# Taking the first queries of a second batch ahead, and a rebuilt opening, in a fused attention and SwiGLU kernel

## The chip, the cores and the metric

The kernel runs on one core of one Trainium2 chip. The metric is the device time of one execution in microseconds (us). In the views PE is TensorE (PEld its weight loads), DVE VectorE, ACT ScalarE, POOL GpSimd and SP SyncE; FFN stands for the SwiGLU block. The kernel before takes 454.88 us (median of 4 runs, 454.54 to 455.0).

## The reference, cut to what matters

Eight batches of eight heads of causal attention with a decay, 576 tokens each, head size 64, feed a SwiGLU block over all 4,608 tokens (model width 512, inner width 1,536).

```python
scores = scale * np.matmul(q, k.transpose(0, 1, 3, 2))
cum = np.cumsum(np.log(np.clip(f, 0.0001, 1.0)), axis=-1)
scores = np.where(causal, -1e9, scores + cum[:, :, :, None] - cum[:, :, None, :])
attn = softmax(scores)                    # rows divided by their sums
x = (attn @ v) as [4608, 512]
out = (silu(x @ w_gate) * (x @ w_val)) @ w_out
```

A token's FFN needs all eight heads of its batch. So the first FFN matmul can only come when the first 256 queries of all eight heads of batch 0 are done. Until then TensorE has only attention, and attention needs the other engines as much as TensorE.

## The kernel before

The program is a list of **slots**, one per step of a head (four per head, 256 in all, then a tail). `at(slot, fn, ...)` puts a piece of work into a slot, every engine executes its own part in program order, and FFN matmuls are mixed in by a ration per slot. Heads go in pairs; `QK[p]` holds the transposed q and k of a pair, with four more rows for the decay, so that the score matmul adds the decay itself. Batch 0 is split: the first 256 queries of its eight heads come first (slots 0 to 7), the rest after.

```python
def rows(p):                                   # decay rows of a later pair, by way of DRAM
    nc.sync.dma_start(out=QK[p % NBUF][D:KR, :, :S],
                      in_=dec_dram[2 * p : 2 * p + 2].rearrange("j w r s -> r (j w) s"))
...
def turn(h, half):                             # batch 0: sums to columns on TensorE, reciprocal,
    ...                                        # and turn_back(): columns to rows, both fp32
def collect(g): ...                            # later batches: sums -> DMA -> reciprocal -> DMA -> broadcast
...
TILES = [(0, QSPLIT), (QSPLIT, MT - QSPLIT)] + [(t0, MT) for t0 in range(MT, N_TOK, MT)]   # 256, 256, 512, ...
...
# opening: the decay is computed for all 64 heads on VectorE, then
for r in range(4):                             # four copies, all batch 0 at once, after the last row is done
    nc.sync.dma_start(out=QKA[D + r : D + r + 1, :, :, :S]..., in_=dec[:H, :, r])
...
def slot(h, i):
    if h >= H:
        return NSLOT * h + i
    return h if i == 0 else H + (NSLOT - 1) * h + i - 1
...
for c in range(4):                             # weights in quarters, from GpSimd
    at(1 + 3 * c, weights, wg, w_gate, lo, hi, True)
    at(2 + 3 * c, weights, wv, w_val, lo, hi, True)
for c in range(4):
    at(15 + 3 * c, weights, wo, w_out, 3 * c, 3 * c + 3, False)
```

The softmax here doesn't subtract the row's maximum and nothing guards it: scores larger than these inputs give would overflow.

## Time and profile before

| what | value |
|---|---|
| time, median | 454.88 us |
| span of the profiled run | 454.3 us |
| TensorE busy | 418.7 us, 92% |
| first score matmul | 19.04 us |
| first FFN (gate) matmul | 37.36 us |
| steady part (slot 192 to 224, one batch) | 45.6 us |

The page of the kernel before, cut to TensorE, its granted clock and the DMA. A row of digits is the span in 40 slices of 11.4 us; a digit is a share in tenths.

```profile
span 454.3 us, 7863 instructions
...
PE 418.7 (92%) x2752; PEld 239.9 (53%) x2752; DVE 290.9 (64%) x504; ACT 264.4 (58%) x537; POOL 185.0 (41%) x418
...
PE   2399999878799999999999999999999999999996
...
PEclk9999999998899999999999999999999999999999
DMA  9799935482746275628462746274614023101002
```

TensorE is full except in the first two slices and around slices 8 to 11. Everything after is saturated, so whatever is to be gained lies before about 125 us.

The windows view of the kernel before, in stretches of 5 us: window, its length, then busy us and instruction count of TensorE, its weight loads, VectorE, ScalarE and GpSimd, then granted clock, DMA share and GB/s.

```profile
15.00:20.00 5.00, 0.96 (x8) 0.87 (x9) 1.62 (x4) 0.45 (x2) 0.00 (x0) 1.00 0.57 139
20.00:25.00 5.00, 4.43 (x33) 3.37 (x30) 3.15 (x6) 3.70 (x9) 4.75 (x11) 1.00 0.66 178
25.00:30.00 5.00, 4.57 (x28) 2.95 (x28) 3.98 (x12) 2.17 (x5) 4.87 (x14) 1.00 1.07 142
35.00:40.00 5.00, 5.00 (x29) 3.50 (x28) 2.13 (x6) 2.22 (x6) 2.51 (x6) 1.00 1.31 202
50.00:55.00 5.00, 5.00 (x47) 3.92 (x47) 4.00 (x11) 2.61 (x7) 3.18 (x7) 1.00 1.07 230
```

GpSimd is full from 20 to 30, and the DMA engines are full from 25 to 55 (a share over 1 means that packets overlap).

The timeline of TensorE in the kernel before: start, duration, line, operation, tiles, and in brackets the idle time before it and what ended it.

```profile
19.04 0.80 PE L157 MATMUL s<-QK 68*128 68x256 bf16 x4 [4.58 <-DMA QK<-dec]
...
37.36 1.04 PE L287 MATMUL gp<-xT,wg 128*128 128x256 bf16 x4
38.19 0.64 PE L296 MATMUL vp<-xT,wv 128*128 128x256 bf16 x2
...
39.09 0.38 PE L296 MATMUL vp<-xT,wv 128*128 128x256 bf16 x2
39.31 0.60 PE L287 MATMUL gp<-xT,wg 128*128 128x256 bf16 x4
```

The first score matmul waits 4.58 us for the decay rows. Two 256-wide matmuls take 0.64 us at 38.19 and 0.38 us at 39.09: TensorE ran at half rate until 39.0. The Trainium skill, "TensorE: Matmul & The Clock Gate", section "Seeing it yourself" in Part 1, warns not to trust the clock records fully; here the durations decide.

### The profile page before, as it was taken

How to read it: one execution, taken by the hardware profiler on the slowest of the kernel's cores; microseconds unless marked ns; L12 is line 12 of the kernel's file. 1: busy time of each engine (PE TensorE's matmuls, PEld its weight loads, DVE VectorE, ACT ScalarE, POOL GpSimd, SP SyncE). 2: the span in 40 equal slices, each digit the busy share in tenths (PEclk: the TensorE clock that was granted, in tenths of full speed). 3: DMA queues.
4: the chain of work that ended last, by engine and by line, in shares of the span. 5: the costliest groups of instructions: out<-in, count | busy, mean ns of one | idle time of the engine just before them, and what ended most of it. 6: DMA issues, size and time to landing. Idle time of an engine off the chain costs nothing.

```text
span 454.3 us, 7863 instructions
## 1 busy us (share of the span) xinstructions
PE 418.7 (92%) x2752; PEld 239.9 (53%) x2752; DVE 290.9 (64%) x504; ACT 264.4 (58%) x537; POOL 185.0 (41%) x418
## 2 busy tenths in 40 slices
PE   2399999878799999999999999999999999999996
PEld 1266756655455555555555555555555544444442
DVE  7575655764569656965696469646964783771770
ACT  5344657786577667666766676667666631332322
POOL 6493535665535354545454545454545200000000
PEclk9999999998899999999999999999999999999999
DMA  9799935482746275628462746274614023101002
GB/s 205 188 173 216 198 76 166 107 183 62 184 105 132 56 202 132 134 54 203 130 135 56 202 131 133 56 203 130 134 28 123 26 55 98 48 0 70 24 0 95
DMA packets 68728, 52.83 MB, mean 116 GB/s; under 512 B 44624, under 2 KB 63056, under 8 KB 67728
## 3 DMA queue, kind: packets, MB, share of 16 engines
q1 hardware_dynamic: 57552, 38.35, 33.5%
q10 hardware_dynamic: 5312, 9.26, 9.4%
q0 software_dynamic: 5824, 4.72, 7.0%
q8 instruction: 22, 0.36, 0.3%
q14 instruction: 18, 0.15, 0.1%
HBM read 46.67 MB, written 10.16 MB: 125 GB/s over the span
## 4 chain that ended last, share of the span: by engine, by line
PE 68%; DVE 15%; DMA 6%; issue 4%; ACT 4%; POOL 2%; POOLq 0%; DVEq 0%; ACTq 0%
PE fo L305 18%; PE gp L287 16%; PE vp L296 15%; PE s L157 7%; DMA rb<-rc_d 4%; DVE hh L298 3%; DVE QK L141 3%; DVE xT L269 3%; DVE th L290 3%; PE tp L134 3%; ACT th L289 1%; PE rs L239 1%; ACT QK L139 1%; ACT pt L163 1%; DMA lf<-in_f_dram 1%
## 5 line engine op out<-in xcount | busy, mean ns | idle before, releaser
L163 ACT ACTIVATE pt<-s 128x384 bf16<-128x384 f32 (+2 forms) x248 | 124.0, 503 | 70.4 <-PE s L157 66.1
L175 POOL TENSOR_SCALAR_AFFINE_SELECT pt<-pt 128x256 bf16<-128x256 bf16 (+2 forms) x248 | 86.3, 350 | 171.3 <-ACT pt L163 169.5
L296 PE MATMUL vp<-xT,wv 128*128 128x512 bf16 (+1 forms) x480 | 124.2, 358 | 0.9 <-DVE th L290 0.5
L287 PE MATMUL gp<-xT,wg 128*128 128x512 bf16 (+1 forms) x480 | 124.3, 360 | 0.5 <-DVE xT L269 0.5
L290 DVE SCALAR_TENSOR_TENSOR th<-th,gp 128x512 f32<-128x512 f32 (+1 forms) x120 | 75.8, 631 | 63.6 <-ACT th L289 62.8
L305 PE MATMUL fo<-wo,hh 128*128 128x512 bf16 x432 | 107.7, 382 | 0.0
L289 ACT ACTIVATE th<-gp 128x512 f32<-128x512 f32 (+1 forms) x120 | 66.4, 554 | 56.3 <-PE gp L287 49.5
L157 PE MATMUL s<-QK 68*128 68x320 bf16 (+4 forms) x448 | 89.4, 271 | 4.6 <-DMA QK<-dec 4.6
L298 DVE TENSOR_TENSOR hh<-th,vp 128x512 bf16<-128x512 f32 (+1 forms) x120 | 75.5, 629 | 6.2 <-PE vp L296 0.9
L157 PEld LDWEIGHTS <-QK 68*128 68x128 bf16 x448 | 44.9, 101 | 46.5 <-issue 5.9
L141 DVE COPY QK<-tp 64x576 bf16<-64x576 bf16 x64 | 48.2, 753 | 29.9 <-PE tp L134 29.3
L296 PEld LDWEIGHTS <-wv 128*128 128x128 bf16 x480 | 45.3, 98 | 36.6 <-issue 2.5
L269 DVE TENSOR_TENSOR xT<-ev,rb 64x576 bf16<-64x576 f32 x56 | 45.1, 805 | 30.4 <-DMA rb<-rc_d 29.8
L287 PEld LDWEIGHTS <-wg 128*128 128x128 bf16 x480 | 44.9, 98 | 33.9 <-issue 0.7
L305 PEld LDWEIGHTS <-hh 128*128 128x128 bf16 x432 | 40.4, 98 | 35.8
L139 ACT ACTIVATE QK<-tp 64x576 bf16<-64x576 bf16 x64 | 41.2, 644 | 2.4 <-PE tp L134 1.9
L308 ACT ACTIVATE ot<-fo 128x512 f32<-128x512 f32 x36 | 21.5, 596 | 36.0 <-PE fo L305 29.7
L193 PEld LDWEIGHTS <-VB_101 128*128 128x128 bf16 x112 | 9.6, 101 | 12.8 <-PE s L157 5.7
L122 POOL CAST b_k_100<-nat_k 96x768 bf16<-96x768 f32 x16 | 16.2, 1012 | 0.0
L134 PE MATMUL tp<-ident,b_q_97 128*128 128x128 bf16 x96 | 9.0, 236 | 5.4 <-POOL b_q_97 L122 5.4
L193 PEld LDWEIGHTS <-VB_103 128*128 128x128 bf16 x112 | 9.6, 98 | 8.1 <-issue 2.4
L122 POOL CAST b_k_99<-nat_k 96x768 bf16<-96x768 f32 x16 | 13.4, 837 | 1.1 <-DMA nat_k<-in_k_dram 1.1
(344 smaller groups left out, 349.6 us busy)
## 6 DMA issues: line engine op xcount, KB each, us to landing
nat_q<-in_q_dram SPq DMA_DIRECT2D x32, 288.0 KB
nat_k<-in_k_dram SPq DMA_DIRECT2D x32, 288.0 KB
out_dram<-ot SPq DMA_DIRECT2D x36, 256.0 KB
nat_v<-in_v_dram SPq DMA_DIRECT2D x64, 128.0 KB
rb<-rc_d ACTq DMA_DIRECT2D x14, 576.0 KB
wg<-in_moe_w_gate_dram POOLq DMA_DIRECT2D x4, 384.0 KB, 7.9
wv<-in_moe_w_val_dram POOLq DMA_DIRECT2D x4, 384.0 KB, 8.6
wo<-in_moe_w_out_dram POOLq DMA_DIRECT2D x4, 384.0 KB, 6.2
```

The source lines that it names most:

```text
L139: nc.scalar.activation(dst, sr, AF.Copy)
L141: nc.vector.tensor_copy(dst, sr)
L157: nc.tensor.matmul(s[:, c : c + w], QK[b][:, 2 * j + 1, kt * P : (kt + 1) * P], QK[b][:, 2 * j, q0 : q0 + w], start=True, stop=True,)
L163: nc.scalar.activation(pt[:, off : off + c], s[:, :c], AF.Exp, scale=0.125)
L175: nc.gpsimd.affine_select(out=diag, in_=diag, pattern=[[1, m]] if m else [[0, 2], [1, P]], compare_op=ALU.is_ge, fill=0.0, base=0, channel ...
L269: nc.vector.tensor_mul(xT[a * D : (a + 1) * D, (h % H) // 2, b0 : b0 + S], E[g][:D, j], RB[g][:, j])
L287: nc.tensor.matmul(g_[:, :n], wg[:, ko, fs], xT[:, ko, ts], start=(ko == 0), stop=(ko == KD - 1))
L289: nc.scalar.activation(th[:, :n], g_[:, :n], AF.Tanh, scale=0.5)
L290: nc.vector.scalar_tensor_tensor(out=th[:, :n], in0=th[:, :n], scalar=1.0, in1=g_[:, :n], op0=ALU.add, op1=ALU.mult)
L296: nc.tensor.matmul(v_[:, :n], wv[:, ko, fs], xT[:, ko, ts], start=(ko == 0), stop=(ko == KD - 1))
L298: nc.vector.tensor_mul(h_[:, :n], th[:, :n], v_[:, :n])
L305: nc.tensor.matmul(o[:m], hh[fc][:, m0 : m0 + m], wo[:, fc, :], start=(fc == 0), stop=(fc == KF - 1))
```

## The change

Its intent: start attention sooner, keep TensorE warm with dummy matmuls, take work from GpSimd in the first heads, and split batch 1 as batch 0 is split, so that FFN tiles of 256 tokens are ready early and fill the stretch in which attention alone cannot fill TensorE. The core of the diff (helper bookkeeping cut, and with it a changed order of the casts, transposes and normalisations of the later batches):

```diff
+AHEAD = 2
...
+    def idle(n):                       # dummy matmuls of 512 columns into a spare PSUM tile
+        for _ in range(n):
+            z = ps_ffn.tile([P, MT], F32, name="z", tag="f")
+            nc.tensor.matmul(z, ident, ident.unsqueeze(1).to_broadcast([P, MT // P, P]), start=True, stop=True)
...
-    def turn(h, half):                 # fp32 transposes for both parts of batch 0
+    def turn(h):                       # for its first part alone; the second goes through the DMA chain
...
-    TILES = [(0, QSPLIT), (QSPLIT, MT - QSPLIT)] + [(t0, MT) for t0 in range(MT, N_TOK, MT)]
+    TILES = [(0, QSPLIT), (QSPLIT, QSPLIT), (2 * QSPLIT, QSPLIT), (3 * QSPLIT, AHEAD * S - 3 * QSPLIT)]
+    TILES += [(t0, min(MT, N_TOK - t0)) for t0 in range(AHEAD * S, N_TOK, MT)]
...
+        def row(r):                    # pair 0 alone, each row when it is computed
+            nc.sync.dma_start(out=QK[0][D + r : D + r + 1, :, :S], in_=dec[0:2, :, r])
...
+        row(3)
+        nc.sync.dma_start(out=dec_dram[:H], in_=dec[:H])
...
+        load(3, "q")
+        load(3, "k")
+        for part in range(3):
+            load(2, "v", part)
+        rows(1)                        # pairs 1 to 3 by way of DRAM
+        rows(2)
+        rows(3)
...
-        for r in range(4):
-            nc.sync.dma_start(out=QKA[D + r : D + r + 1, ...], in_=dec[:H, :, r])
...
+        nc.sync.dma_start(out=dec_dram[H:], in_=dec[H:])
...
     def slot(h, i):
-        if h >= H:
+        if h >= AHEAD * H:
             return NSLOT * h + i
-        return h if i == 0 else H + (NSLOT - 1) * h + i - 1
+        b, j = h // H, h % H
+        return NSLOT * H * b + (j if i == 0 else H + (NSLOT - 1) * j + i - 1)
...
+    for part in range(3):
+        at(0, load, 3, "v", part)
+    for n in range(first):
+        at(n, idle, 1)
...
-        at(1 + 3 * c, weights, wg, w_gate, lo, hi, True)
-        at(2 + 3 * c, weights, wv, w_val, lo, hi, True)
+        at(-1 + 3 * c, weights, wg, w_gate, lo, hi, True)
+        at(0 + 3 * c if c else -1, weights, wv, w_val, lo, hi, True)
```

## The prediction

> **What bounds it now.** The page gives TensorE 418.7 busy of 454.3 us (92%), so the time is TensorE's work plus the stretches where it waits or runs slow. Windows and timeline show four stages.
> 1. 0 to 19.0 us: no real matmul. The first score matmul waits for four copies of decay rows into QK, which start only after the VectorE chain ends at 12.1 us and take from 11.6 to 17.2 to issue.
> 2. 19.0 to 37.4: first queries of batch 0, up to the first gate matmul. GpSimd is saturated (9.6 of 10 us from 20 to 30), and TensorE is cold: four 256-wide gate matmuls take 1.04 us at 37.4, 0.60 soon after. The Trainium skill, "TensorE: Matmul & The Clock Gate", Part 1, says that the array runs at half rate until about 3.4 us of sustained work; these durations agree, although the granted-clock column says 1.0.
> 3. 37.4 to 123.9 (first 512-wide FFN tile): FFN work is rationed, 256 tokens over 48 program slots. Attention alone sets 0.92 us per slot (7.35 us per two heads). From 60 to 125 TensorE idles about 10.5 us, and the granted clock falls to 0.73 (105 to 110) and 0.66 (120 to 125), about 3 us more. VectorE waits for the broadcast reciprocals (1.4 and 4.0 us) begin the worst gaps.
> 4. From 123.9: regular, 45.56 us per batch (1.42 per slot), TensorE 98.8% busy. The change leaves this rate alone.
>
> **What the change does.**
> - Pair 0's rows go out singly, for two heads, as each is computed: first score matmul at about 15 instead of 19 (-4).
> - GpSimd loses, in the first heads, one of two masks per head, two blankings and two casts; 40 dummy matmuls (8.5 us if warm) keep TensorE warm. First gate matmul at about 29.5, some 14.5 us of first heads instead of 18.4 (-4).
> - Batch 0's second parts use the DMA chain instead of fp32 transposes on TensorE. Timeline starts give 0.25 + 0.49 us per head: -6.
> - Batch 1's first 256 queries go ahead; the first tiles are 256, 256, 256, 384. Counted in the built instruction streams, FFN work per slot becomes 0.38 us (slots 12-52), 0.96 (52-84), 0.60 (84-122), then 0.96 as before. Only the first stays under the 0.92 us attention limit. Estimate from 0.92 and 1.42: slot 52 near 68, 84 near 114, 122 near 155, where before it was at 176 (123.9 + 37 x 1.42), with 3 us more FFN done. Idle and throttle of stage 3 shrink by about 8 us.
> - FFN columns stay equal (276.5 us at full rate); 256-wide matmuls start every 0.11 us, so small tiles cost TensorE nothing.
>
> **Sum.** -4 -4 -6 -8 and -2 for cold FFN matmuls: -24. All of it is on the critical path, as TensorE is saturated afterwards. Predicted 430.5 us, 8 in 10 between 421 and 441. Faster by over 2%: 0.94; within: 0.05; slower: 0.01.
>
> **What would show it.** First score matmul 14 to 16 us; first gate matmul 28 to 31; 256-wide gate groups of four at about 0.6 from the start; TensorE idle between 40 and 130 under 6 us; clock 1.0 throughout; steady period still 45.5 us; tail after the last matmul still 3.6 us.
>
> **What would make it wrong.** Weights and batch 1's loads share the DMA with the new sum chains at 40 to 60 us, where DMA is already full (share over 1 from 25 to 55): the in-order VectorE would wait for reciprocals and stop everything, and the clock could drop. Pair 1's rows go through DRAM and may be late (1 to 3 us). If slots 12-52 run at 1.1 us, 7 us are lost.

## More of the kernel before

The DMA issues of the weights in the kernel before: count, KB of one, and median us from issue to landing.

```profile
wg<-in_moe_w_gate_dram POOLq DMA_DIRECT2D x4, 384.0 KB, 7.9
wv<-in_moe_w_val_dram POOLq DMA_DIRECT2D x4, 384.0 KB, 8.6
wo<-in_moe_w_out_dram POOLq DMA_DIRECT2D x4, 384.0 KB, 6.2
```

## The result, and the profile after

The changed kernel takes 452.43 us (median; 451.59, 452.25 and 452.6 in its fast runs). The ratio to the kernel before is 0.9941, with a 95% interval of 0.9922 to 0.9961: the same within 2%. It is 22 us above the prediction and 11 us above its upper end. Every ratio here is the mean time of one kernel's fast runs over that of the kernel before in the same rounds, so it is not quite the ratio of the medians that are quoted beside it.

One of the changed kernel's runs, the profiled one, took 723.46 us at a granted clock of 0.559. It was in the slow state, it is not explained, and no comparison below uses it; all 72 runs of the experiments were fast. The profile after is that of a second, fast profiled execution of the unedited changed kernel (the run `e1_again`, span 450.9 us).

The page of the changed kernel, the same rows:

```profile
span 450.9 us, 8053 instructions
...
PE 416.5 (92%) x2803; PEld 247.2 (55%) x2840; DVE 290.0 (64%) x523; ACT 267.5 (59%) x551; POOL 174.3 (39%) x409
...
PE   7399387899899899999999999999999999999996
...
PEclk9879889999999999999999999999999999999999
DMA  9899961670818554943584359435922222100201
```

The holes of slices 8 to 11 are smaller, but there are two new ones: a 3 in the second slice and a 3 in the fifth. The clock row dips beside both.

The windows of the changed kernel, the same columns:

```profile
15.00:20.00 5.00, 0.23 (x2) 0.00 (x0) 0.45 (x1) 0.73 (x2) 4.71 (x12) 0.85 1.03 254
20.00:25.00 5.00, 4.60 (x28) 3.18 (x28) 2.10 (x4) 2.74 (x6) 4.45 (x8) 0.50 0.85 117
25.00:30.00 5.00, 5.00 (x32) 3.32 (x31) 3.79 (x10) 2.54 (x6) 1.84 (x4) 0.63 1.25 214
...
50.00:55.00 5.00, 0.00 (x0) 0.00 (x0) 0.00 (x0) 0.36 (x1) 0.86 (x2) 0.76 1.15 225
```

TensorE does nothing from 15 to 20 and again from 50 to 55, with the DMA full both times; from 20 to 28.7 it runs at half rate. GpSimd is relieved only from 25 on (1.84 instead of 4.87 us).

The timeline of TensorE in the changed kernel at the lines that answer to those of before:

```profile
13.95 0.34 PE L166 MATMUL s<-QK 68*128 68x256 bf16 x2 [1.66 <-DMA QK<-dec]
...
20.40 0.48 PE L166 MATMUL s<-QK 68*128 68x256 bf16 x2 [5.17 <-DMA QK<-dec_d]
...
36.59 0.60 PE L293 MATMUL gp<-xT,wg 128*128 128x256 bf16 x4
...
55.34 0.80 PE L135 MATMUL tp<-ident,b_k 128*128 128x128 bf16 x6 [6.03 <-ACT QK L142]
```

The first pair starts 5 us sooner, at 13.95. The second pair then waits 5.17 us for its own decay rows, which come through DRAM (`dec_d`), and starts at 20.40, where it was before. The first gate matmul comes at 36.59 instead of 37.36.

The other new hole ends at 55.34. ScalarE, which TensorE waited for, in the timeline:

```profile
54.06 0.53 ACTq L250 DMA_DIRECT2D sc<-ev  x1
54.64 0.65 ACT L142 ACTIVATE QK<-tp 64x576 bf16<-64x576 bf16 x1 [5.63 <-DMA nat_q<-in_q_dram]
```

And GpSimd, in the timeline:

```profile
54.14 0.82 POOL L122 CAST b_q<-nat_q 96x768 bf16<-96x768 f32 x1 [4.92 <-DMA nat_q<-in_q_dram]
```

And the chain of waits over that stretch (start, us, what):

```profile
41.58 12.41 DMA nat_q<-in_q_dram
...
54.06 0.53 ACTq L250
...
54.64 0.66 ACT QK L142
...
55.34 0.80 PE tp L135 x6
```

All three name one transfer: the q of a pair of batch 1, issued at 41.58, took 12.41 us to land; the median of such loads over the run is 3.9 us. GpSimd needs it for its next cast. ScalarE does not need its data at all there: it stands at the issue of a DMA of its own (`sc<-ev`), because the semaphore that this issue takes in the built program is one that the earlier load still holds. The trace shows it: the load of 41.58 and the issue at 54.06 carry the same semaphore, and ScalarE waits for it just before the issue. ScalarE works in order, so its copy of a TensorE result (to `QK`) behind that issue waits, and TensorE behind the copy.

The DMA issues of the weights in the changed kernel:

```profile
wg<-in_moe_w_gate_dram POOLq DMA_DIRECT2D x4, 384.0 KB, 11.6
wv<-in_moe_w_val_dram POOLq DMA_DIRECT2D x4, 384.0 KB, 13.6
wo<-in_moe_w_out_dram POOLq DMA_DIRECT2D x4, 384.0 KB, 9.4
```

Each weight quarter takes 3 to 5 us longer than before. Batch 1's loads are not the main reason: in e9, an experiment told below in which batch 1 is not ahead, the quarters take nearly as long. No run isolates what the reason is.

```profile
wg<-in_moe_w_gate_dram POOLq DMA_DIRECT2D x4, 384.0 KB, 10.8
wv<-in_moe_w_val_dram POOLq DMA_DIRECT2D x4, 384.0 KB, 12.2
wo<-in_moe_w_out_dram POOLq DMA_DIRECT2D x4, 384.0 KB, 9.8
```

### Where each kernel stands at the same program slot

The start of a slot is read from the trace as the first weight load of its score matmuls, counted in program order. FFN work done is the count of FFN columns issued by then, at 2,400 columns per us; the trace agrees to about 1% (six 512-wide matmuls take 1.46 us and one 0.38 us, so five more take 0.216 us each, 2,370 per us). The last three columns are experiments told below. Every column is one profiled execution, and the four runs of one version differ by 1 to 4.4 us in whole time, so a difference of a few tenths of a us between columns says nothing.

| at slot | before | changed | predicted | batch 1 not ahead (e9) | mended (e17) | mended, batch 1 not ahead (e18) |
|---|---|---|---|---|---|---|
| 0, us | 19.0 | 14.0 | 15 | 13.8 | 13.3 | 14.0 |
| 12, us | 36.5 | 36.0 | 29.5 | 36.7 | 32.3 | 33.0 |
| 52, us | 85.5 | 85.3 | 68 | 79.7 | 78.9 | 74.1 |
| 84, us | 118.7 | 135.0 | 114 | 115.5 | 128.6 | 109.3 |
| 122, us | 176.0 | 178.5 | 155 | 167.8 | 172.1 | 161.4 |
| 255, us | 364.4 | 365.0 | | 353.8 | 357.8 | 347.1 |
| FFN done by slot 52, us | 20.2 | 15.4 | | 15.4 | 15.4 | 15.4 |
| FFN done by slot 84, us | 30.5 | 46.1 | | 32.6 | 46.1 | 32.6 |
| FFN done by slot 122, us | 66.3 | 69.1 | | 66.6 | 69.1 | 66.6 |
| whole time, us | 454.88 | 452.43 | 430.5 | 447.97 | 446.28 | 440.35 |

(The prediction's 29.5 is for the first gate matmul, which is at slot 12 to within 1 us.) The changed kernel reaches slot 122 2.5 us later than the kernel before, with 2.8 us more FFN work behind it. Up to there the whole change is worth nothing. The little it gains comes afterwards: slots 122 to 255 take 186.4 us instead of 188.4.

### The profile page after: what moved, and what is told of

Its sections match the earlier page's. It is cut to its first block, busy times and chain, and to the rows that moved or that the text cites. A ratio compares the mean times of both kernels' runs of the same rounds, so it can differ in the third digit from the quotient of the medians.

```text
span 721.7 us, 8090 instructions
## 1 busy us (share of the span) xinstructions
PE 711.6 (99%) x2840; PEld 341.5 (47%) x2840; DVE 300.0 (42%) x523; ACT 276.5 (38%) x551; POOL 170.1 (24%) x409
## 2 busy tenths in 40 slices
DMA packets 70195, 53.52 MB, mean 74 GB/s; under 512 B 45834, under 2 KB 64266, under 8 KB 69322
## 4 chain that ended last, share of the span: by engine, by line
PE 95%; DMA 3%; DVE 0%; SPq 0%; ACT 0%; POOL 0%; issue 0%; ACTq 0%
PE gp L293 23%; PE fo L311 23%; PE vp L302 23%; PE s L166 10%; PE tp L135 5%; DMA nat_v<-in_v_dram 2%; DMA nat_k<-in_k_dram 1%; PE z L150 1%; SPq L98 0%; PE rs L239 0%; ACT QK_98 L142 0%; PE o_565 L198 0%; PE o_1528 L198 0%; PE o_659 L198 0%; PE o_2235 L198 0%; PE o_1229 L198 0%
## 5 line engine op out<-in xcount | busy, mean ns | idle before, releaser
L302 PE MATMUL vp<-xT,wv 128*128 128x512 bf16 (+2 forms) x528 | 204.4, 514 | 0.0
L293 PE MATMUL gp<-xT,wg 128*128 128x512 bf16 (+2 forms) x528 | 204.3, 511 | 0.0
L311 PE MATMUL fo<-wo,hh 128*128 128x512 bf16 x432 | 182.9, 581 | 0.0
L296 DVE SCALAR_TENSOR_TENSOR th<-th,gp 128x512 f32<-128x512 f32 (+2 forms) x132 | 78.0, 591 | 192.8 <-ACT th L295 192.6
L295 ACT ACTIVATE th<-gp 128x512 f32<-128x512 f32 (+2 forms) x132 | 68.5, 519 | 132.4 <-PE gp L293 130.3
L302 PEld LDWEIGHTS <-wv 128*128 128x128 bf16 x528 | 69.5, 136 | 70.4 <-issue 59.4
L304 DVE TENSOR_TENSOR hh<-th,vp 128x512 bf16<-128x512 f32 (+2 forms) x132 | 77.9, 590 | 40.8 <-PE vp L302 35.8
L274 DVE TENSOR_TENSOR xT<-ev,rb 64x576 bf16<-64x576 f32 (+2 forms) x72 | 50.5, 702 | 1.9 <-DMA rb<-rc_d 0.9
L166 PE MATMUL s<-QK_97 68*128 68x320 bf16 (+4 forms) x112 | 31.5, 363 | 2.9 <-DMA QK_97<-dec_d 2.9
L166 PE MATMUL s<-QK_96 68*128 68x320 bf16 (+4 forms) x112 | 32.4, 373 | 0.0
L166 PE MATMUL s<-QK_99 68*128 68x320 bf16 (+4 forms) x112 | 32.1, 368 | 0.0
L166 PE MATMUL s<-QK_98 68*128 68x320 bf16 (+4 forms) x112 | 32.0, 370 | 0.0
L166 PEld LDWEIGHTS <-QK_97 68*128 68x128 bf16 x112 | 15.2, 136 | 24.3 <-issue 22.5
L166 PEld LDWEIGHTS <-QK_96 68*128 68x128 bf16 x112 | 14.8, 132 | 23.9 <-issue 23.3
L166 PEld LDWEIGHTS <-QK_99 68*128 68x128 bf16 x112 | 15.1, 134 | 22.1 <-issue 20.2
L166 PEld LDWEIGHTS <-QK_98 68*128 68x128 bf16 x112 | 13.7, 122 | 24.2 <-issue 22.6
```

The lines of the kernel that those rows point to most:

```text
L166: nc.tensor.matmul(s[:, c : c + w], QK[b][:, 2 * j + 1, kt * P : (kt + 1) * P], QK[b][:, 2 * j, q0 : q0 + w], start=True, stop=True,)
L274: nc.vector.tensor_mul(xT[a * D : (a + 1) * D, (h % H) // 2, b0 : b0 + n], E[g][:D, c : c + n], RB[x][:, j * n : (j + 1) * n])
L293: nc.tensor.matmul(g_[:, :n], wg[:, ko, fs], xT[:, ko, ts], start=(ko == 0), stop=(ko == KD - 1))
L295: nc.scalar.activation(th[:, :n], g_[:, :n], AF.Tanh, scale=0.5)
L296: nc.vector.scalar_tensor_tensor(out=th[:, :n], in0=th[:, :n], scalar=1.0, in1=g_[:, :n], op0=ALU.add, op1=ALU.mult)
L302: nc.tensor.matmul(v_[:, :n], wv[:, ko, fs], xT[:, ko, ts], start=(ko == 0), stop=(ko == KD - 1))
```

## The experiments

The first theory was another one: that the dense dummies bring on a stretch of low granted clock, which eats the gain. e1 to e3 tested it. The trace of e1 shows half rate for 10.2 and 6.8 us only, each time after a long wait, and without the dummies the time is no better. So the theory from e4 on: two waits for DMA, each followed by a stretch at half rate, eat the gain. The first is for pair 1's decay rows (15 to 20 us), the second for batch 1's loads behind the weights (49 to 55 us). Rivals: the dummies cost more than they give; ScalarE's in-order DMA issue alone makes the second wait; taking batch 1 ahead is itself a loss, whatever the loads do.

### The dummies: e1, e2 and e3 (before 455.01 us)

Unedited again:

> The changed kernel unedited, to get a profile of a fast run. All theories: about 452 us. Throttle theory (the first theory): most of the missing 20 us is a stretch of granted clock below 1.0 in the first 130 us; a mean clock near 0.977 over 450 us, if the low grade is 0.56 as in the slow run, is about 24 us of throttle, worth 10 to 11 us against 3 to 4 before. Stall theory (the rival): the clock is near 1.0 until 100 us and TensorE waits show the missing time: late decay rows of pair 1, weights, reciprocal chains.

Without the dummies:

> The changed kernel without the 40 dummy matmuls. Theory A (the dense dummy matmuls at the start bring on the throttle): no clock of 0.56 in the first 40 us, no slow run of 720 us, time 440 to 447. Theory B (the dummies do what they are meant to): TensorE cold through the first heads, time 453 to 458. If the throttle comes from the later fuller stages, the spell stays and the time is within 2 us of the changed kernel.

```diff
-        for _ in range(n):
+        for _ in range(0):
```

The kernel before, with `idle()` and the same 40 dummies at the same places, and nothing else of the change:

> The kernel before with the same 40 dummy matmuls in the same places. Theory A: a throttled stretch appears near the start that the kernel before has not, time 456 to 465, perhaps a run far slower. Theory B: TensorE warm in the first heads, first gate matmul 2 to 3 us earlier, time 451 to 453.

```diff
+        idle(9)
         transposes(0, "q")
+        idle(2)
...
         transposes(0, "k")
+        idle(7)
         transposes(1, "q")
+        idle(4)
         cast(0, "v")
         transposes(1, "k")
+        idle(6)
...
+    for n in range(12):
+        at(n, idle, 1)
```

| run | median, us | ratio to before | 95% |
|---|---|---|---|
| e1_again | 451.6 | 0.9925 | 0.9899 to 0.9951 |
| e2_no_dummies | 452.43 | 0.9945 | 0.9924 to 0.9966 |
| e3_before_dummies | 451.28 | 0.992 | 0.9892 to 0.9947 |

Inside the changed kernel the dummies are worth about 1 us, which the intervals do not tell from nothing; in its trace TensorE is at half rate again from 18.5 us on, in the 5-us wait for pair 1's rows. Alone, in the kernel before, they bring 3.7 us: as much as the whole change. In e3 TensorE is warm from 5.8 to 12.6 us and, but for one spell at 118, from 22.8 on, and slot 12 comes 1.2 us, slot 52 2.3 us and slot 122 3.5 us sooner than before.

### The two waits, one at a time: e4 to e7 (before 455.94 us)

Pair 1's rows direct as well, not by way of DRAM:

> The changed kernel, but pair 1's decay rows also go straight from the decay tile as each is computed, not through DRAM behind other loads. Stall theory: the 5.2 us TensorE wait for the rows of pair 1 at 15.2 us falls under 1 us, the cold spell from 18.8 to 29.0 us goes, the first gate matmul is near 29 to 30 us instead of 36.6, and the time is 443 to 446. Rival (the wait only moves, the first heads are bound by something else, or the gain is lost in the full DMA at 40 to 55 us): first gate matmul earlier but slot 52 still at about 85 us, time 449 to 452.

```diff
-            nc.sync.dma_start(out=QK[0][D + r : D + r + 1, :, :S], in_=dec[0:2, :, r])
+            for p in range(2):
+                nc.sync.dma_start(out=QK[p][D + r : D + r + 1, :, :S], in_=dec[2 * p : 2 * p + 2, :, r])
...
-        rows(1)
```

The output weights later:

> The changed kernel, but the four loads of the down-projection weights are issued in slots 26 to 32 instead of 15 to 24. Theory (DMA full of weights makes batch 1's early query loads late, 12.5 us from issue to landing, and ACT, GpSimd and then TensorE stop for it): the 6.0 us TensorE wait at 49 us shrinks to under 2 us and its cold spell (52.9 to 59.8 us) goes, slot 52 at 77 to 79 us instead of 85.3, time 443 to 446. Rival (the wait is the lane rule or another order, not bandwidth): stall stays, time 451 to 453.

```diff
-        at(15 + 3 * c, weights, wo, w_out, 3 * c, 3 * c + 3, False)
+        at(26 + 2 * c, weights, wo, w_out, 3 * c, 3 * c + 3, False)
```

The issue that ScalarE stood at, moved to GpSimd for the first two sum chains:

> The changed kernel, but the first two copies of sums (the start of the reciprocal chain) are issued by GpSimd instead of ACT, where the first stood 5 us waiting for the semaphore lane of a query load. Lane theory (ACT stuck in a lane wait is the whole stall): the 6.0 us TensorE wait at 49 us goes, time 443 to 446. Bandwidth theory (the query load itself is late, and GpSimd waits for it anyway with the masks behind it): TensorE still waits 4 us or more near 49 to 54 us, time 449 to 453.

```diff
-        nc.scalar.dma_start(
+        (nc.gpsimd if x < 2 else nc.scalar).dma_start(
             out=SC[x][:, :c], in_=E[g][D : D + 1, GH * lo : GH * (lo + n)]
```

The first two together:

> Both edits, pair 1's rows straight from the decay tile and late down-projection weights. If the two stalls are separate, the gains add: 435 to 439 us, slot 52 near 70 us as predicted for the change. If the earlier start only makes the DMA shortage worse: 443 to 447.

| run | median, us | ratio to before | 95% | slot 0, us | slot 12, us | slot 52, us |
|---|---|---|---|---|---|---|
| e4_direct_pair1 | 452.19 | 0.9928 | 0.9877 to 0.998 | 15.5 | 40.9 | 84.0 |
| e5_late_wo | 449.14 | 0.9845 | 0.9794 to 0.9896 | 13.7 | 36.3 | 82.0 |
| e6_pool_collect | 453.16 | 0.9946 | 0.9892 to 0.9999 | 13.8 | 37.9 | 85.0 |
| e7_direct_late | 451.69 | 0.9913 | 0.9859 to 0.9968 | 15.5 | 40.1 | 82.9 |

e4 missed, and is the most instructive of them. Pair 1's wait of 5.17 us is gone, but it is replaced by waits of 3.6 us (pair 0's rows, which now queue with twice as many) and 2.2 us (pair 2's rows). The loss is then in the clock. The windows of e4:

```profile
25.00:30.00 5.00, 4.92 (x27) 3.27 (x28) 2.95 (x9) 2.01 (x4) 1.52 (x3) 0.50 1.22 219
...
35.00:40.00 5.00, 5.00 (x23) 2.79 (x23) 2.08 (x7) 1.31 (x3) 1.86 (x4) 0.50 1.22 235
```

TensorE is busy nearly all of this time and still at half rate, until 41.6 us; 23 matmuls fill 5 us. So slot 12 comes 4.8 us later than in the unedited kernel. A removed wait can thus be paid for twice over by a longer stretch at half rate. By slot 52 it is more than made up (84.0 against 85.3): slots 12 to 52 take 43.1 us instead of 49.3, with every weight still loaded, and TensorE meets no wait over 1.5 us there.

e5 shortens TensorE's wait at 49 us from 6.0 to 3.0 us and brings about 3 us (2.5 by the medians of e1 and e5, 3.6 by their ratios): part of the second wait is the output weights. e6 brings nothing: another wait of 3.5 us shows up at 57 us. GpSimd now stood for the q load (9.48 us to landing) and issued the sums at 53.29, these took 5.90 us to land, and ScalarE stood at its next DMA issue, which comes after them in the chain of the sums. Whoever stands still, late transfers are at the root of it. e7 shows that the gains do not add: its interval overlaps both e5's and that of the unedited kernel.

### Warm from the start, and without batch 1 ahead: e8 and e9 (before 454.94 us)

e8 is e7 with more reordering to keep TensorE warm: loads of pair 3 and the rows of pairs 2 and 3 issued sooner, GpSimd's blanking of buffers and the weights a little later, 14 dummies instead of 6 ahead of slot 0 and three per slot in slots 0 to 4.

> The last kernel (pair 1 direct, late down-projection weights) with the start mended further: loads of pair 3 earlier, rows of pairs 2 and 3 right after the decay tile is written, fewer GpSimd instructions before the first mask, and more dummies in the waits, so that TensorE does not fall to half rate. Warm theory (the first heads are bound by TensorE at half rate, and the later slots follow the start): clock 1.0 from 8 us on, first gate matmul at 28 to 32 us instead of 40.6, slot 52 at 72 to 76 us instead of 82.9, time 439 to 444. DMA theory (all loads of both batches and the weights must pass first, and slots 20 to 52 are paced by it): first gate matmul earlier but slot 52 stays within 3 us of 83, time 448 to 452.

```diff
         row(1)
+        load(3, "q")
+        load(3, "k")
...
         nc.sync.dma_start(out=dec_dram[:H], in_=dec[:H])
+        rows(2)
+        rows(3)
...
-        idle(6)
+        idle(14)
...
-    at(0, blanks, 3)
+    at(0, nc.gpsimd.tensor_copy, ident_f, ident)
+    at(1, blanks, 2)
+    at(2, blanks, 3)
     for n in range(first):
-        at(n, idle, 1)
+        at(n, idle, 3 if n < 5 else 1)
...
-        at(-1 + 3 * c, weights, wg, w_gate, lo, hi, True)
-        at(0 + 3 * c if c else -1, weights, wv, w_val, lo, hi, True)
+        at(3 * c, weights, wg, w_gate, lo, hi, True)
+        at(1 + 3 * c, weights, wv, w_val, lo, hi, True)
```

e9 is the changed kernel with only batch 0 split, as before; the opening is the changed one.

> The changed kernel with only batch 0's first queries ahead: batch 1 in plain order with its loads and transposes spread as in later batches, first tiles 256 and 320, then 512 from token 576 on. If the denser preparation of batch 1 in slots 12 to 52 costs as much as the fuller tiles give back: the 6 us wait at 49 us goes, slot 52 at 77 to 80 us, but slots 60 to 110 are short of FFN work again, time 449 to 454. If taking batch 1's first queries ahead is what gives the gain: 456 to 462.

```diff
-AHEAD = 2
+AHEAD = 1
...
-    TILES = [(0, QSPLIT), (QSPLIT, QSPLIT), (2 * QSPLIT, QSPLIT), (3 * QSPLIT, AHEAD * S - 3 * QSPLIT)]
+    TILES = [(0, QSPLIT), (QSPLIT, AHEAD * S - QSPLIT)]
```

| run | median, us | ratio to before | 95% | slot 12, us | slot 52, us |
|---|---|---|---|---|---|
| e8_warm_start | 450.52 | 0.9896 | 0.9852 to 0.994 | 40.2 | 83.5 |
| e9_ahead1 | 447.97 | 0.9833 | 0.9799 to 0.9867 | 36.7 | 79.7 |

e8 starts slot 0 late, at 17.3 us, and has a half-rate spell of 3.4 us from 18.5; it still reaches slot 8 at 30.0 us, 1 us sooner, and then meets a new wait of 4.12 us: pair 3's V, loaded from slot 0 on, lands late, and VectorE, in order, holds the reciprocals behind its cast. TensorE goes to half rate again, at 32.2 us. e9 is the surprise: taking the headline idea of the change out makes it faster, by 0.9 points of ratio, and it is ahead by slot 52 (79.7 against 85.3, with the same 15.4 us of FFN done).

### Is it the loads? A quarter of the weights: e10, e11 and e12 (before 456.52 us)

These load only the first quarter of each weight and use it for all four, so the results are wrong (relative error 1.74 in e10), while the matmuls and their order stay. GpSimd is relieved a little too: it issues 3 weight loads instead of 12, at about 0.8 us each. e10 does so in the changed kernel, e11 in e8, and e12, the control, in the kernel before.

> The changed kernel with only the first quarter of each weight loaded and used four times over: same instructions and shapes on all compute engines, a quarter of the weight traffic, a wrong result on purpose. DMA theory (the first 60 us are paced by loads waiting behind the weights): the 6 us wait at 49 us goes, slot 52 at 70 to 77 us instead of 85.3, time 437 to 444. Rival (the slots 12 to 52 are bound by the engines preparing batch 1 twice as densely): slot 52 at 79 us or later, time 446 to 451.

> The kernel with the mended, warm start and a quarter of the weight traffic, a wrong result on purpose. If the clock at the start and the DMA together are what the prediction missed: first gate matmul at 28 to 32 us, slot 52 at 68 to 73 us, time 431 to 438, about what was predicted for the change. If the engines bound slots 12 to 52 anyway: slot 52 at 74 to 79, time 439 to 445.

> Control: the kernel before with a quarter of the weight traffic, a wrong result on purpose. DMA theory: before loads batch 1 later and waits little for loads, so less than 3 us: 451 to 455. If all kernels gain alike from lighter weights (7 us or more), the weights do not explain the difference between them.

```diff
-                fs = slice(fc * P, (fc + 1) * P)
+                fs = slice(fc % 3 * P, (fc % 3 + 1) * P)
...
-                    nc.tensor.matmul(o[:m], hh[fc][:, m0 : m0 + m], wo[:, fc, :],
+                    nc.tensor.matmul(o[:m], hh[fc][:, m0 : m0 + m], wo[:, fc % 3, :],
...
-    for c in range(4):
+    for c in range(1):
```

(The last edit is made at both loops over the weights.)

| run | median, us | ratio to before | 95% | slots 12 to 52, us |
|---|---|---|---|---|
| e10_quarter_after | 446.41 | 0.9775 | 0.973 to 0.982 | 42.5 |
| e11_quarter_warm | 448.74 | 0.9797 | 0.9751 to 0.9842 | 42.9 |
| e12_quarter_before | 455.91 | 0.9979 | 0.9947 to 1.001 | 49.9 |

In the changed kernel the hole at 49 us is gone, and slots 12 to 52 take 42.5 instead of 49.3 us, with the order of the program unchanged. But e10 enters the stretch 1.9 us later (slot 12 at 38.0), so slot 52 comes 4.8 us sooner, at 80.5. The ratio falls by 1.5 points. In e8's opening the same relief brings 1.0 point, and slot 52 only 0.9 us (82.6 in e11). In the kernel before, three quarters less weight traffic brings nothing that the interval can tell from zero. So the weights cost nothing as such: in the changed kernel's order they make a load late that TensorE comes to need, and how much that costs depends on when TensorE arrives. e4, with all weights, passes the same slots in 43.1 us because it arrives 4.8 us later. The Trainium skill, "Trainium Kernel Development and Optimization", section "Key Constraints", says that DMAs issued from the SP, ACT and POOL queues run on the same 16 DMA engines and interleave. This trace agrees: weights issued by GpSimd and q loads issued by SyncE overlap from 41 to 55 us at a DMA share over 1, and the q load takes 12.41 us.

### Mending the opening: e13 to e16

e13 is e9 with the late output weights of e5 (before 456.52 us). e14 is e13 with 24 dummies in slot 1, to bridge the wait for pair 1's rows; e15 is the changed kernel with those dummies alone; e16 is e15 with a quarter of the weights (wrong). The last three: before 456.43 us.

> The version with only batch 0 ahead, plus late down-projection weights, a right result, a candidate that beats both. If both reliefs of the DMA add up: 444 to 446.5 us. If the wait at 50 to 56 us in it comes from the gate and value weights alone: 447 to 448.5.

> The version with only batch 0 ahead and late down-projection weights, with 24 instead of 1 dummy matmuls in slot 1, which fill the wait for the rows of pair 1 (about 15.2 to 20.3 us) and so keep TensorE's clock up. Right result, candidate for the best. Warm theory: no half-rate spell before 30 us, slot 12 at 32 to 34 us instead of 37.8, time 442 to 445. Rival (the heads then wait for the next load): slot 12 at 36 to 38, time 446 to 448.

> The changed kernel with 24 instead of 1 dummy matmuls in slot 1, nothing else. Warm theory: no half-rate spell from 18.5 to 28.7 us, slot 12 at 32 to 34 us instead of 36.0; what comes of it later depends on the loads: if the wait at 49 us only grows by what was won, the time stays at 450 to 452; if not, 447 to 449.

> The changed kernel with the 24 dummies in slot 1 and a quarter of the weight traffic, a wrong result on purpose: both suspected causes of slots 0 to 52 relieved. If they are the causes and add: slot 12 at 32 to 34 us, slot 52 at 74 to 77 us, time 440 to 443. If slot 52 stays at 80 us or later, the engines' own pace or the remaining loads bound it.

```diff
     for n in range(first):
-        at(n, idle, 1)
+        at(n, idle, 24 if n == 1 else 1)
```

| run | median, us | ratio to before | 95% | slot 12, us |
|---|---|---|---|---|
| e13_ahead1_late | 446.58 | 0.9782 | 0.9749 to 0.9814 | 37.8 |
| e14_ahead1_late_fill | 447.54 | 0.981 | 0.9768 to 0.9853 | 38.6 |
| e15_fill | 451.84 | 0.9917 | 0.9875 to 0.996 | 38.4 |
| e16_quarter_fill | 448.73 | 0.9843 | 0.9795 to 0.989 | 39.0 |

e13 lies 0.5 points of ratio below e9. The dummies of the other three bring nothing to the whole time (e14 against e13, e15 against e1, e16 against e10). They do what they should: full rate lasts to about 30 us in all three, and slot 8 comes at 28.4 us in e16 instead of 31.0. Then the wait that e8 had met comes again. VectorE in e16:

```profile
31.42 0.43 DVE L119 CAST VB<-nat_v 128x512 bf16<-128x512 f32 x1 [3.84 <-DMA nat_v<-in_v_dram]
```

And TensorE in e16:

```profile
32.67 0.63 PE L239 MATMUL rs<-ident_f,rcp 128*64 128x128 f32 x2 [3.72 <-DVE rcp L234]
```

TensorE is then at half rate from 30.6 to 40.8 us, and slot 12 is no sooner for all the warmth. That it happens with a quarter of the weights too says that the other three quarters are not what makes this load late; the first quarters of gate and value weights, issued at 17.3 and 18.2 us beside it, are still there. The V loads took 8.6 to 10.6 us in e16. Their rows are 256 bytes long (64 floats) in DRAM. The Trainium skill, "DMA: Bandwidth & Descriptors", section "Specifications", gives 512 bytes as the least transfer for line rate; the page of the changed kernel counts 45,834 of 70,195 packets below that. No run here made the rows longer, so that is a plausible reason, not a shown one. What all the runs up to here had in common is that pair 3's V is issued from slot 0, behind the write of the decay rows of 56 heads to DRAM (issued at 17.2 us in e16).

### Pair 3's V ahead of that write: e17 and e18 (before 456.36 us)

e17 is the changed kernel with three edits: the 24 dummies, the late output weights, and pair 3's V loaded right after `rows(3)`, ahead of the write. e18 is the same three edits with batch 1 not ahead.

> The changed kernel with the 24 dummies in slot 1, late down-projection weights, and pair 3's V loaded before the large write of the other decay rows. Load-wall theory (with the clock up, slot 8 stands 3.7 us for pair 3's V, which lands at 31.4 us, and TensorE then falls to half rate): that wait falls under 1.5 us, no half-rate spell before 40 us, slot 12 at 32 to 35 us instead of 38.4, slot 52 at 76 to 79 us, time 442 to 446. If the V still lands after 31 us: slot 12 at 37 or later, time 448 to 452.

> The same three edits in the version with only batch 0 ahead, a candidate for the best. Load-wall theory: slot 12 at 32 to 35 us instead of 38.6, time 441 to 444. If the V still lands late: 446 to 448. Against the run beside it, it tells again what taking batch 1 ahead costs or gives once the start runs warm: 3 to 5 us slower with batch 1 ahead, if its denser preparation is what costs.

```diff
         rows(3)
+        for part in range(3):
+            load(3, "v", part)
         cast(2, "q")
...
-    for part in range(3):
-        at(0, load, 3, "v", part)
...
-        at(n, idle, 1)
+        at(n, idle, 24 if n == 1 else 1)
...
-        at(15 + 3 * c, weights, wo, w_out, 3 * c, 3 * c + 3, False)
+        at(26 + 2 * c, weights, wo, w_out, 3 * c, 3 * c + 3, False)
```

| run | median, us | ratio to before | 95% | slots 12 to 52, us | 52 to 84 | 84 to 122 |
|---|---|---|---|---|---|---|
| e17_fill_v3 | 446.28 | 0.9792 | 0.9755 to 0.983 | 46.6 | 49.7 | 43.5 |
| e18_ahead1_fill_v3 | 440.35 | 0.9653 | 0.9618 to 0.9687 | 41.1 | 35.2 | 52.1 |
| the same less the columns of all matmuls in it, at 2,400 per us, e17 | | | | 15.5 | 6.0 | 4.5 |
| the same less its columns, e18 | | | | 10.2 | 4.6 | 2.3 |

The opening is mended in both: slot 12 at 32.3 and 33.0 us, full rate to 49.2 us in e17 and from 6.8 to 436.8 us of 438.9 in e18. One of V's two large loads can be timed in each of e15 and e17: in e15 it is issued at 18.06 us and lands at 28.48, in e17 it is issued at 17.24 and lands at 23.08. e18 differs from e14 in the place of these three loads alone, and takes 440.35 us instead of 447.54, beside a kernel before of 456.36 and 456.43: once the dummies keep TensorE warm, the place of these three loads is worth 7.2 us. No run tells whether the write ahead of it or the later issue as such made it late, and none moved the V without the dummies. The row of the granted clock on the page of e18:

```profile
PEclk9999999999999999999999999999999999999999
```

What is left of the second wait, in the windows of e17:

```profile
45.00:50.00 5.00, 1.65 (x16) 1.23 (x15) 0.84 (x2) 1.54 (x4) 2.28 (x6) 0.92 1.10 234
50.00:55.00 5.00, 4.11 (x29) 3.10 (x28) 3.21 (x8) 2.64 (x6) 2.75 (x6) 0.74 0.52 87
```

And the same windows of e18:

```profile
45.00:50.00 5.00, 4.93 (x49) 4.00 (x47) 3.39 (x10) 4.20 (x10) 3.58 (x10) 1.00 0.70 147
50.00:55.00 5.00, 3.67 (x36) 2.90 (x35) 2.23 (x6) 2.58 (x7) 4.86 (x10) 1.00 1.16 201
```

In e17 TensorE is busy for 1.65 of 5 us where it is busy for 4.93 in e18. It waits there for another q load of batch 1, as the chain of waits of e17 shows:

```profile
36.61 10.80 DMA nat_q<-in_q_dram
...
47.48 0.54 ACTq L250
...
48.77 0.49 PE tp L135 x6
```

The two kernels differ in nothing but the splitting of batch 1, with the times of its loads and preparation, and the FFN tiles that follow from it, and that is worth 5.9 us, on the same chip. e18 is the best version found: 3.5% below the kernel before, and correct. It is also the only one that is clearly faster than the kernel before by 2%; the intervals of e5, e9 to e11, e13, e14, e16 and e17 reach across that mark, and the others end short of it. It keeps the rebuilt opening and drops the idea after which the change is named.

## Why the prediction was wrong

The prediction said 430.5 us (421 to 441), faster by over 2% with a chance of 0.94. It measured 452.43. Point by point:

- **The first score matmul at 14 to 16 us: right.** It came at 13.95.
- **"First gate matmul at about 29.5": wrong, 36.6.** This is the first step that failed, by about 7 us: the "-4 -4" of the sum. The prediction took the 5 us won at slot 0 as won for all pairs. But a stretch is as fast as the wait that ends last in it: pair 1's rows still came through DRAM and arrived at about 20.3 us. The prediction named that risk ("1 to 3 us"); it was 5.17 us of idle time, plus 10 us at half rate that the idle time caused. Bridging it (e15, e16) showed a second blocker behind, pair 3's V, and brought nothing by itself. With both taken away (e17) slot 12 comes at 32.3, so 3 us of the miss are neither of these two.
- **"Only the first stays under the 0.92 us attention limit", "slot 52 near 68": wrong, 85.3.** Slots 12 to 52 took 49.3 us instead of 38.5. Of these 10.8 us, about 6.8 are the late q load and the half rate after it, which are gone in e10 and also, with all weights, in e4. The other 4.0 are the pace itself: 42.5 us for 40 slots is 1.06 us per slot where the prediction has 0.96, from its limit of 0.92, and e4 (43.1), e7 (42.8) and e11 (42.9), which pass the stretch under other conditions, come to the same. The limit of 0.92 was read from a regular stretch of the kernel before (7.3 to 7.4 us per eight slots between slots 40 and 68). Why it is not reached is not shown: e18, without batch 1 ahead, still takes 41.1 us, 1.03 per slot. The prediction's last lines named both risks (the full DMA, and "if slots 12-52 run at 1.1 us, 7 us are lost"), and still gave 0.94 to faster by over 2%.
- **Slots 52 to 84 near 46 us and 84 to 122 near 41: 49.7 and 43.5.** Another 3.7 and 2.5 us. With the two errors above they make the 23.5 us by which slot 122 is late (178.5 against 155).
- **"Idle and throttle of stage 3 shrink by about 8 us": wrong in sum.** The windows give TensorE 15.48 busy of 16 us from 36 to 52 before and 11.55 after, where the 6-us wait begins. The holes between 90 and 125 did shrink, as predicted (105 to 110: 3.66 us busy at a clock of 0.73 before, 5.00 at 1.00 after). From 40 to 130 together, TensorE's idle time rose from 11.4 to 15.7 us; the prediction had said under 6.
- **Gate groups of four at 0.6 from the start: right**, 0.60 at 36.59. **Clock 1.0 throughout: wrong**, half rate from 18.5 to 28.7 and from 52.6 to 59.5.
- **FFN 3 us further ahead at slot 122: right**, 69.1 against 66.3. **Steady part unchanged: nearly**; it fell from 45.6 to 45.0 us per batch, as the mean of three batches; it lies at 44.8 to 45.4 in every version with the new code, e2 and e9 too, and at 45.6 in the old, e3 and e12 included. No run isolates why; over slots 122 to 255 it is 1.9 us, most of what the change gained.
- **"All of it is on the critical path": the assumption under the sum.** The sum of gains was made stage by stage as if each stage would end where its own work ends. Each gain in TensorE's work instead ran into a load that had been early enough before.

What the runs show of the cause in one line: of the 24 us, the opening's share is lost to two late transfers (rows of pair 1, then V of pair 3) and the half rate that follows each; and taking batch 1 ahead is a net loss of 5.9 us even with those mended.

What stays open: why batch 1 ahead costs that much. In slots 12 to 52, where e17 takes 5.5 us longer than e18, it has one TensorE wait of 3.35 us that ends at 48.8 (behind another q load of 10.80 us) and a half-rate spell of 3.4 us after it; by estimate these come to some 5 us, but e18 has a wait of 2.9 us of its own there. Slots 52 to 122 also lose 3.6 us more than in e18. That the transposes of eight heads and the copies of their results fall into 16 slots is an argument from the program; no run changed that alone. The slow run of 723 us is not explained either.

The clock deserves its own word. The Trainium skill, "TensorE: Matmul & The Clock Gate", section "What's actually happening" in Part 1, gives half rate after an idle window of about 3.4 us and full rate after as long a busy one. The traces agree in part. The 32 half-rate spells that the fast profiles record before the tail last 3.41 us or a multiple of it, up to eight times; 15 last one such step, so there the return is as stated. In the changed kernel the fall agrees as well: the last matmul ends at about 15.2 us and half rate begins at 18.5. But a fall can come with less idle time: in e10 half rate begins at 31.1, inside a wait of 1.62 us, after 3.4 us in which TensorE was busy for about two thirds. And early in the program the return takes longer: after 20.40 us in the changed kernel TensorE is busy 4.60 of 5 us, and full rate comes at 28.7, 8.3 us later; in e4 it takes from 25 to 41.6 us at a busy share near 0.95, and in the kernel before, by its durations, from 19 to 39, the stretch that the prediction had put down to the 3.4 us. Part 4 of the same page, "PE-mode transpose", says that transposes do not count as busy in the same way. These stretches hold many of them, so it would fit; no run here took them out. The prediction counted an idle gap at its own length; half rate made it cost more.

## What to carry to other kernels

When an opening is bound by several transfers, the gain of making one of them early ends at the next that was just early enough before, so list every transfer that lands in the stretch, with its landing time, before adding up the gains. Work brought forward into a stretch where the DMA share is already above 1 brings its loads with it; price those loads and the in-order engines behind them, not only the TensorE time that it fills. Mending one wait can bring nothing until the next is mended too: the dummies alone brought nothing here, and with one load moved the same version gained 7.2 us. A wait on TensorE of a few us at the start costs its own length plus the stretch at half rate after it, so an experiment that removes a wait must also be read in the clock (here 5.17 us of waiting were followed by 10.2 us at half rate).

## What the Trainium skill lacked or had wrong

- "TensorE: Matmul & The Clock Gate", section "What's actually happening": about 3.4 us of sustained work to full rate, and as long an idle window to half rate. Of 32 half-rate spells 15 lasted 3.41 us; the others lasted 6.8 to 27.3 us. In the changed kernel 8.3 us of work at a busy share over 0.9 passed before full rate, and in e4 over 16 us. And in e10 a wait of 1.62 us was enough for the fall. The page would help by saying how a mix of small score matmuls, transposes and weight loads is counted.
- The same page, section "Seeing it yourself", warns of the clock records, but not of this form: a profile shows a clock of 1.00 until its first record (39.0 us in the kernel before), while durations show half rate (0.64 against 0.38 us for the same two matmuls).
- "DMA: Bandwidth & Descriptors" warns that two DMAs in flight on one semaphore are a danger to the data; no page has the cost of keeping them apart, that an issue can stand still for a transfer that it does not depend on, when the program gives both the same semaphore: ScalarE stood 5.63 us for a q load that was GpSimd's next input and not its own.
- "DMA: Bandwidth & Descriptors" has bandwidth by size, and that each engine takes turns between the queues, but no landing times when the queues compete: here a q load of 288 KB took 3.9 us in the median and 12.41 us among weight quarters, and the gate quarters went from 7.9 to 11.6 us.
- No page that I found explains a single-core run at a clock of 0.559 for the whole program (723.46 us instead of 452, with records of 0.555 and 0.5 alone), seen once.
